# Second-layer products four steps behind the first layer instead of two, from token block 1 on

## The chip, the cores and the metric

The kernel runs on one core of one Trainium2 chip. The metric is the device time of one execution in microseconds. TensorE does the matrix products (PE, its weight loads PEld), VectorE (DVE), ScalarE (ACT) and GpSimd (POOL) the elementwise work, and SyncE (SP) issues the DMA transfers.

## The reference, cut to what matters

Causal attention with a decay, then two MLPs, all in float32. 2304 tokens in rows of 512, 32 heads of 64.

```python
x = attention(q, k, v, f)              # 4 x 8 heads, 576 tokens -> (2304, 512)
h = x @ w_in                           # first layer, 512 -> 2048
g = h * np.tanh(np.where(h > 20.0, h, np.log1p(np.exp(np.minimum(h, 20.0)))))
x2 = g @ w_out                         # second layer, 2048 -> 512
h2 = x2 @ w2_in                        # second stage, 512 -> 1024
solu = h2 * softmax(h2)
out = (layer_norm(solu) * g_ln) @ w2_out   # 1024 -> 512
```

## The kernel before

Every float32 operand is split into a high and a low half in float16, and each product is three matmuls: high by high, high by low, low by high. The tokens are worked off in nine blocks of 256 (`TB`, `NBLK`), the 2048 columns of the first MLP in 16 chunks of 128 (`NF1`). So there are 144 steps n, one for each block and chunk, and the main loop of `emit` runs over half steps `hn`.

In step n, `up(n)` is the first layer: 12 matmuls (L754) into a half of a PSUM tile `h`, which holds two steps and has two buffers (`psh`). After each pair p of steps the activation is computed in three parts. `mish_a(p)` reads `h` on ScalarE into `ta` and `th` (L766, L767; two buffers each). `mish_b(p)` does VectorE (L771), three ScalarE functions (L772 to L774) and VectorE again (L775). `mish_c(p)` casts the high half of the result on ScalarE (L780) and subtracts it on GpSimd for the low half (L781), into `gt`, of which there are three (`GB = 3`).

`down(n)` is the second layer: six matmuls (L798), three for each half of the block's tokens, that add chunk n to two PSUM banks `x2_0` and `x2_1`. Below, "product n" is the six matmuls of `down(n)`. Each bank has one buffer. After the last chunk of a block `evac` scales a bank into `x2h` (L826 on ScalarE, L827 on VectorE, one buffer) and writes it to memory (L828). The next block's first product into a bank waits for that.

Attention runs beside it in slots: scores (L410, L411, L413), exponentials on ScalarE (L454, L469), split on GpSimd (L493), a DMA transpose, and products with the values (L524 to L526). A slot also loads and converts raw tiles of q, k and v. When attention is over, the memory that it held is given to `Stage2`, which loads and splits the weights of the second stage, and the second MLP begins: `first(t)` for a tile of 128 tokens (24 matmuls, L997), normalisation, a transpose of z, `second(t)` (24 matmuls, L1037).

What decides when `down(n)` is issued is the line with `tgt` in the main loop: before, `down` follows two steps behind `up` everywhere (both branches give n - 2). A product is only issued once its `gt` exists, and `mish_c(p)` stands in step 2p + 2. The Tile framework then reorders instructions: it gives each a rank by this program order, and takes the first that is ready in its own model of the times. Each engine works off its own resulting queue in order.

Of the kernel before, what the change touches and what calls it, by code (L numbers as in the profile page):

```python
# [24 lines left out]
NF1 = DFF // P  # L25
# [15 lines left out]
WPF = 2  # L41
S2P = 1
EB = 190
DL = 2
A0 = 16
XB = 3
S2A = 10
# [160 lines left out]
def emit(tc, q, k, v, f, w_in, w_out, w2_in, w2_out, g_ln, out):  # L208
# [427 lines left out]
    def slot_pre():  # L636

        n = pos["k"] - 1
        if 0 <= n < len(seq):
            step_r(*seq[n])  # L640

    def slot_mid():
        n = pos["k"] - 1
        if 0 <= n < len(seq):
            step_h(*seq[n])
# [9 lines left out]
    def slot_pe():  # L655
        n = pos["k"]
        if n < len(seq):
            step_s(*seq[n])
            b, i, hs = seq[n]
            for h in hs:  # L660
                ahead(b, i, h)
        pvs(n - LAG)
        pos["k"] += 1

    def slot():
        slot_pre()
        slot_mid()
        if pos["k"] == n0:
            pvs(n0 - 1)
        slot_pe()  # L670
# [3 lines left out]
    for x in range(len(order) + WPF):  # L674
        if WPF <= x < len(order):
            wsteps.append((order[x][0].load, order[x][1]))
        if x >= WPF:
            w, n = order[x - WPF]
# [5 lines left out]
    def wgo(n):  # L684
        for _ in range(n):
            if wsteps:
                f, a = wsteps.pop(0)
                f(a)
                wdone.add((f, a))
# [54 lines left out]
    def up(n):  # L744
        j, fi = divmod(n, NF1)
        if fi % 2 == 0:
            hps[n // 2] = psh.tile([P, 2, TB], F32, tag="h", name=f"h_{j}_{fi}")
        ph = hps[n // 2][:, fi % 2]
        x = xT[j]
        m = 0  # L750
        for lw, lx in ((0, 0), (0, 1), (1, 0)):
            for c in range(NC1):
                col = lw * 512 + (fi % 4) * P
                nc.tensor.matmul(  # L754
                    ph, win[:, (fi // 4) * NC1 + c, col:col + P], x[:, lx * NC1 + c, :],
                    start=(m == 0), stop=(m == 3 * NC1 - 1))
                m += 1

    def mish_a(p):
        j, fi = divmod(2 * p, NF1)  # L760
        ph = hps.pop(p)
        ta = mp.tile([P, 2, TB], F32, tag="ta", name=f"ta_{p}")
        th = mp.tile([P, 2, TB], F32, tag="th", name=f"th_{p}")
        tmp[p] = (ta, th)
        for b, a, e in segs(j):
            nc.scalar.activation(ta[:, :, a:e], ph[:, :, a:e], AF.Exp, scale=usc(b, fi // 4))  # L766
        nc.scalar.activation(th, ph, AF.Copy, scale=ths[:, fi // 4:fi // 4 + 1] if j else -0.4 * HSC)  # L767

    def mish_b(p):
        ta, th = tmp[p]  # L770
        nc.vector.tensor_scalar(ta, ta, E20, 1.0, op0=ALU.min, op1=ALU.add)  # L771
        nc.scalar.activation(ta, ta, AF.Square)  # L772
        nc.scalar.activation(ta, ta, AF.Ln, scale=0.2, bias=c_k1)
        nc.scalar.activation(ta, ta, AF.Exp, scale=-1.0)  # L774
        nc.vector.scalar_tensor_tensor(th, ta, 2.5, th, op0=ALU.subtract, op1=ALU.mult)  # L775

    def mish_c(p):
        ta, th = tmp.pop(p)
        gt = mp.tile([P, 2, 2, TB], F16, tag="gt", name=f"gt_{p}", bufs=GB)
        nc.scalar.copy(gt[:, 0], th)  # L780
        nc.gpsimd.tensor_tensor(gt[:, 1], th, gt[:, 0], op=ALU.subtract)  # L781
        gts[p] = gt
# [76 lines left out]
    def att_slots(n):  # L859

        j, r = divmod(n, 2 * NF1)
        goal = cum[-1] * min(1.0, (n + 1) / EB)
        x = n0 + LAG + sum(c <= goal + 1e-6 for c in cum[1:])
        lo = need[j + 1] + LAG if j + 1 < NBLK and r >= 2 * NF1 - ATE else 0
        if j == 0:
            lo = max(lo, n0 + LAG + min(need[1] - n0, (r + 1) * (need[1] - n0) // A0))
        hi = need[j + XB] - 1 if j + XB < NBLK else len(seq) + LAG
        return min(max(x, lo), hi)

    NF = NBLK * NF1  # L870
# [1 line left out]
    done = {"d": 0}  # L872
    st2 = None

    for hn in range(2 * (NF + 5)):
        n, half = divmod(hn, 2)
        live = n < NF
        att_now = live and pos["k"] < att_slots(hn)
        if att_now:
            slot_pre()  # L880
        if half == 0:
            if n % 2 == 0 and 0 <= n // 2 - 1 < NF // 2:
                mish_b(n // 2 - 1)
            if att_now:
                slot_mid()
            if live:
                while n < NF1 and (w1_split, n // 4 * 2 + 1) not in wdone:
                    wgo(1)
                up(n)
        else:  # L890
            if live and n % 2:
                while n > NF1 and wsteps:
                    wgo(1)
                mish_a(n // 2)
            if n % 2 == 0 and 0 <= n // 2 - 1 < NF // 2:
                mish_c(n // 2 - 1)
            if att_now:
                slot_mid()
            tgt = n - 2 if (n > DL + 8 or n >= NF) else n - DL
            while done["d"] < min(tgt, NF):  # L900
                if done["d"] // 2 not in gts:
                    break
                while done["d"] < NF1 and (w2_split, done["d"] // 2) not in wdone:
                    wgo(1)
                down(done["d"])
                done["d"] += 1
        if att_now:
            slot_pe()
        wgo(WS1)
        while live and pos["k"] < att_slots(hn):  # L910
            slot()
        if half and wstp is not None and not wsteps:
            wstp.close()
            wstp = None
        if st2 is None and half and pos["k"] >= len(seq) + LAG:
            ea.close()
            st2 = Stage2(tc, es, w2_in, w2_out, g_ln, x2d, us2, out, ones)
            st2n = n
        if st2 is not None:
            if hn % S2E == 0:  # L920
                st2.prepare(S2P)
            if half and n > st2n + S2A and (n - S2A) % S2B == 0 and st2.ready():
                st2.step(TT * (done["d"] // NF1))
# [165 lines left out]
```

## Time and profile before

| | us |
|---|---|
| median of three runs | 861.46 |
| lowest and highest of them | 859.14, 862.57 |
| the profiled execution | 862.0 |
| its span in the trace | 860.2 |

| engine | busy us | share |
|---|---|---|
| TensorE (matmuls) | 748.2 | 87% |
| VectorE | 606.7 | 71% |
| ScalarE | 549.1 | 64% |
| GpSimd | 442.2 | 51% |

Busy is the time in which an engine worked on something; idle time stands before the instruction that ended it, with what released it ("<-"). Matmuls overlap, so their mean duration is longer than the time from one to the next.

### The profile page before, as it was taken

How to read it: one execution, taken by the hardware profiler on the slowest of the kernel's cores; microseconds unless marked ns; L12 is line 12 of the kernel's file. 1: busy time of each engine (PE TensorE's matmuls, PEld its weight loads, DVE VectorE, ACT ScalarE, POOL GpSimd, SP SyncE). 2: the span in 40 equal slices, each digit the busy share in tenths (PEclk: the TensorE clock that was granted, in tenths of full speed). 3: DMA queues.
4: the chain of work that ended last, by engine and by line, in shares of the span. 5: the costliest groups of instructions: out<-in, count | busy, mean ns of one | idle time of the engine just before them, and what ended most of it. 6: DMA issues, size and time to landing. Idle time of an engine off the chain costs nothing.

```text
span 860.2 us, 16457 instructions
## 1 busy us (share of the span) xinstructions
PE 748.2 (87%) x6174; PEld 477.6 (56%) x6174; DVE 606.7 (71%) x1158; ACT 549.1 (64%) x1202; POOL 442.2 (51%) x341
## 2 busy tenths in 40 slices
PE   0555777789899988999999999986999999999997
PEld 0444545557567665676757677554555554444443
DVE  6699998597667878858887755599566444665451
ACT  5555657868778786888886767686955554333331
POOL 2268676755876576776678753228733122022110
PEclk9999997789999999999999999999999999999999
DMA  9999554487897889898896632841023423344543
GB/s 237 208 246 271 166 174 92 87 157 120 149 190 157 154 152 161 178 191 140 164 184 124 138 67 56 221 172 62 26 38 79 81 59 75 89 98 104 108 88 81
DMA packets 328571, 114.88 MB, mean 134 GB/s; under 512 B 317676, under 2 KB 317676, under 8 KB 328492
## 3 DMA queue, kind: packets, MB, share of 16 engines
q1 hardware_dynamic: 328492, 113.84, 63.2%
q8 instruction: 48, 0.79, 0.4%
q14 instruction: 31, 0.25, 0.1%
HBM read 46.59 MB, written 9.55 MB: 65 GB/s over the span
## 4 chain that ended last, share of the span: by engine, by line
PE 40%; DVE 23%; DMA 13%; ACT 9%; issue 8%; POOL 7%; SPq 1%; POOLq 0%; DVEq 0%; ACTq 0%
PE h L997 10%; PE o L1037 10%; PE x L798 9%; PE h L754 7%; DMA pT<-ph 4%; POOL ph L493 4%; DVE th L775 3%; DVE ta L771 2%; DMA w2i_r<-in_moe_w_in_dram 1%; DVE wout L140 1%; PE pv L524 1%; DVE ph L490 1%; DVE wout L138 1%; POOL gt L781 1%; DMA rawk<-in_k_dram 1%
## 5 line engine op out<-in xcount | busy, mean ns | idle before, releaser
L798 PE MATMUL x<-wout,gt 128*128 128x512 f16 x864 | 222.1, 392 | 21.8 <-ACT gt L780 10.1
L754 PE MATMUL h<-xT,win 128*128 128x256 f16 x1728 | 223.3, 279 | 2.3 <-POOL win L202 1.7
L493 POOL TENSOR_TENSOR ph<-p,ph 128x512 f16<-128x512 f32 (+4 forms) x120 | 159.6, 1334 | 80.3 <-ACT ph L492 32.8
L754 PEld LDWEIGHTS <-win 128*128 128x128 f16 x1728 | 170.3, 100 | 45.3 <-POOL win L202 1.8
L781 POOL TENSOR_TENSOR gt<-th,gt 128x512 f16<-128x512 f32 x72 | 91.9, 1277 | 100.5 <-ACT gt L780 100.5
L798 PEld LDWEIGHTS <-gt 128*128 128x128 f16 x864 | 81.6, 100 | 103.7 <-issue 14.9
L1025 POOL TENSOR_TENSOR z<-sl,z 128x1024 f16<-128x1024 f32 x18 | 38.7, 2150 | 138.1 <-DVE s2c L1004 111.3
L997 PE MATMUL h<-w,x2T 128*128 128x512 f16 x432 | 98.4, 380 | 2.9 <-POOL w L205 1.6
L1037 PE MATMUL o<-wo,zT 128*128 128x512 f16 x432 | 96.5, 379 | 0.5 <-DMA zT<-z 0.5
L410 PE MATMUL sp<-kt,qa 128*128 128x128 f16 (+3 forms) x480 | 71.8, 225 | 21.1 <-ACT p L454 11.9
L454 ACT ACTIVATE p<-sp,nm 64x64 f32<-64x64 f32 (+7 forms) x128 | 61.2, 484 | 41.0 <-DVE nm L452 23.3
L524 PE MATMUL pv<-vt,pT 128*128 128x64 f16 (+3 forms) x480 | 71.0, 203 | 15.4 <-DMA pT<-ph 10.7
L775 DVE SCALAR_TENSOR_TENSOR th<-ta,th 128x512 f32<-128x512 f32 x72 | 69.4, 965 | 21.1 <-ACT ta L774 20.9
L780 ACT CAST gt<-th 128x512 f16<-128x512 f32 x72 | 44.3, 615 | 48.6 <-DVE th L775 47.2
L411 PE MATMUL sp<-kt,qb 67*128 67x128 f16 (+3 forms) x480 | 72.9, 226 | 2.6 <-DVE qb L399 2.6
L997 PEld LDWEIGHTS <-x2T 128*128 128x128 f16 x432 | 42.3, 98 | 53.9 <-issue 4.0
L525 PE MATMUL pv<-vt,pT 128*128 128x64 f16 (+3 forms) x480 | 70.1, 198 | 1.0 <-DVE vt L198 1.0
L1037 PEld LDWEIGHTS <-zT 128*128 128x128 f16 x432 | 42.2, 98 | 51.5 <-DMA zT<-z 1.0
L526 PE MATMUL pv<-vt,pT 128*128 128x64 f16 (+3 forms) x480 | 70.3, 198 | 0.0
L772 ACT ACTIVATE ta<-ta 128x512 f32<-128x512 f32 x72 | 45.3, 631 | 36.0 <-DVE ta L771 35.8
L524 PEld LDWEIGHTS <-pT 128*128 128x128 f16 (+3 forms) x480 | 45.6, 102 | 36.7 <-DMA pT<-ph 20.5
L771 DVE TENSOR_SCALAR ta<-ta 128x512 f32<-128x512 f32 x72 | 53.7, 745 | 16.6 <-ACT ta L766 16.2
(235 smaller groups left out, 1455.8 us busy)
## 6 DMA issues: line engine op xcount, KB each, us to landing
wi_r<-in_moe_w_in_dram SPq DMA_DIRECT2D x8, 1024.0 KB
wo_r<-in_moe_w_out_dram SPq DMA_DIRECT2D x8, 1024.0 KB
rawk<-in_k_dram SPq DMA_DIRECT2D x25, 256.0 KB
rawv<-in_v_dram SPq DMA_DIRECT2D x25, 256.0 KB
x2d<-x2h SPq DMA_DIRECT2D x18, 256.0 KB
out_dram<-ro SPq DMA_DIRECT2D x18, 256.0 KB
w2i_r<-in_moe_w_in_dram SPq DMA_DIRECT2D x4, 1024.0 KB
w2o_r<-in_moe_w_out_dram SPq DMA_DIRECT2D x4, 1024.0 KB
```

Source lines behind the costliest of these rows:

```text
L410: nc.tensor.matmul(o, qa[:, h, r0:r1_], kc[:, h, a0:a1], start=True, stop=False)
L411: nc.tensor.matmul(o, qb_[:67, h, r0:r1_], kc[:67, H + h, a0:a1], start=False, stop=(c != i))
L493: nc.gpsimd.tensor_tensor(p4[:, :, 1], pv3, p4[:, :, 0], op=ALU.subtract)
L524: nc.tensor.matmul(o, pT[a0:a1, k, :m], vh, start=(c == 0), stop=False)
L526: nc.tensor.matmul(o, pT[a0:a1, k + 1, :m], vh, start=False, stop=(c == i))
L754: nc.tensor.matmul(ph, win[:, (fi // 4) * NC1 + c, col:col + P], x[:, lx * NC1 + c, :], start=(m == 0), stop=(m == 3 * NC1 - 1))
L771: nc.vector.tensor_scalar(ta, ta, E20, 1.0, op0=ALU.min, op1=ALU.add)
L775: nc.vector.scalar_tensor_tensor(th, ta, 2.5, th, op0=ALU.subtract, op1=ALU.mult)
L781: nc.gpsimd.tensor_tensor(gt[:, 1], th, gt[:, 0], op=ALU.subtract)
L798: nc.tensor.matmul(o, gt[:, lg, n % 2, t * P:(t + 1) * P], wout[:, fi, lw * 512:(lw + 1) * 512], start=(first and m == 0), stop=(last and ...
L997: nc.tensor.matmul(h[:, half * 512:(half + 1) * 512], x[:, lx * NC1 + c, :], self.w2[:, half * NC1 + c, lw * 512:(lw + 1) * 512], start=(n ...
L1037: nc.tensor.matmul(o, zT[:, lz * NF2 + c, :], self.wo[:, c, lw * 512:(lw + 1) * 512], start=(n == 0), stop=(n == 3 * NF2 - 1))
```

## The change

From step 20 on (`NF1 + 4`), `down` follows four steps behind `up`; in steps 20 and 21 no product is issued while the distance grows. The constant `DL` becomes `DL2 = 4`, and the loop has two steps more at its end for the last products. Block 0's products keep their distance.

```diff
-DL = 2
+DL2 = 4
...
-    for hn in range(2 * (NF + 5)):
+    for hn in range(2 * (NF + DL2 + 3)):
...
-            tgt = n - 2 if (n > DL + 8 or n >= NF) else n - DL
+            tgt = n - 2 if n < NF1 + 4 else n - DL2
```

Since the framework orders by rank, the four queues differ from product 22 on. Three places show it. Names end in a number of the build; `gt_45` holds products 90 and 91, `h_5_14` is the first layer of block 5, chunks 14 and 15.

TensorE at product 90, before (four of its six matmuls stand ahead of the rest of `h_5_14`):

```order
L798 LDWEIGHTS gt_45_7155
L798 MATMUL x2_5_1_0_6663<-wout_94,gt_45_7155 128x512
L754 LDWEIGHTS win_93
L754 MATMUL h_5_14_7191<-xT_5_4301,win_93 128x256
L754 LDWEIGHTS win_93
```

TensorE at product 90, now (the last of its six matmuls, and what follows):

```order
L798 LDWEIGHTS gt_45_7143
L798 MATMUL x2_5_1_0_6771<-wout_94,gt_45_7143 128x512
L754 LDWEIGHTS win_93
L754 MATMUL h_6_0_7236<-xT_6_5177,win_93 128x256
L754 LDWEIGHTS win_93
```

Product 90 moved behind the whole of `h_5_14` and runs in one piece; the next block's `h_6_0` follows it.

ScalarE at the end of block 1, before (`x2h_2` and `x2h_3` empty the two banks of block 1; `qn_2_0`, `kn0` and `vt_2_0` convert raw tiles of the next batch; `nm_1_4` belongs to attention):

```order
L469 ACTIVATE p32_1_129,rsum_1_4_3318<-sp0_146,nm_1_4_1_3369 128x512
L826 ACTIVATE x2h_3_3224<-x2_1_1_0_2155,x2m_3_3218 128x512
L780 CAST gt_17_3360<-th_17_3306 128x512
L766 ACTIVATE ta_18_3445<-h_2_4_3334,usc1_0_79 128x2x64
L766 ACTIVATE ta_18_3445<-h_2_4_3334,usc1_1_80 128x2x192
```

ScalarE there, now:

```order
L767 ACTIVATE th_19_3572<-h_2_6_3458,ths_91 128x512
L197 ACTIVATE qn_2_0_3531<-rawq_2_0_3480,scu_2_3392 64x8x64
L197 ACTIVATE kn0_124<-rawk_2_0_3482,scu_2_3392 64x8x64
L197 ACTIVATE vt_2_0_3537<-rawv_2_0_3484,scv_2_3395 64x512
L826 ACTIVATE x2h_3_3350<-x2_1_1_0_2155,x2m_3_3344 128x512
L772 ACTIVATE ta_19_3571<-ta_19_3571 128x512
```

The emptying of the second bank moved from ahead of the cast of pair 17 to behind the first part of pair 19 and behind three conversions of raw tiles.

SyncE there, before (`x2d` is the write of `x2h` to memory):

```order
L300 DMA rawq_2_0_3492<-in_q_dram 64x8x64
L498 DMA_TRANSPOSE pT_1_3_6_3234<-ph_1_3_6_3164 128x16x128
L828 DMA x2d_95<-x2h_2_3212 128x1024
L300 DMA rawk_2_0_3494<-in_k_dram 64x8x64
L300 DMA rawv_2_0_3496<-in_v_dram 64x8x64
L828 DMA x2d_95<-x2h_3_3224 128x1024
```

SyncE there, now:

```order
L300 DMA rawq_2_0_3480<-in_q_dram 64x8x64
L300 DMA rawk_2_0_3482<-in_k_dram 64x8x64
L300 DMA rawv_2_0_3484<-in_v_dram 64x8x64
L828 DMA x2d_95<-x2h_2_3338 128x1024
L498 DMA_TRANSPOSE pT_1_4_0_3362<-ph_1_4_0_3294 128x20x128
L551 DMA_TRANSPOSE xT_3_2923<-xh_1_3_3427 128x8x128
L396 DMA_TRANSPOSE qa_2_0_3534<-qn_2_0_3531 128x8x64
L300 DMA rawq_2_1_3775<-in_q_dram 128x8x64
L374 DMA_TRANSPOSE kt_2_0_3527<-kn0_124 128x8x64
L300 DMA rawk_2_1_3777<-in_k_dram 128x8x64
L828 DMA x2d_95<-x2h_3_3350 128x1024
```

The first write moved behind two raw loads and the second behind six more issues.

## Rows read from the trace of the kernel before

**Rows 1.** The page's head: span, busy us, share and instructions of each engine.

```profile
span 860.2 us, 16457 instructions
PE 748.2 (87%) x6174; PEld 477.6 (56%) x6174; DVE 606.7 (71%) x1158; ACT 549.1 (64%) x1202; POOL 442.2 (51%) x341
```

**Rows 2.** Windows: stretch and length, busy us of PE, PEld, DVE, ACT, POOL, PEclk, DMA.

```profile
0.00:237.00 237.00, 158.49 (x1488) 115.44 (x1489) 195.44 (x334) 154.73 (x348) 147.88 (x107) 0.91 0.78 173
237.00:537.00 300.00, 284.07 (x3043) 201.35 (x3042) 222.01 (x415) 232.82 (x562) 198.10 (x178) 0.99 0.80 147
537.00:606.00 69.00, 55.80 (x362) 35.14 (x360) 57.59 (x90) 49.94 (x88) 28.42 (x18) 0.98 0.47 145
606.00:856.00 250.00, 249.52 (x1288) 125.64 (x1285) 131.71 (x320) 110.90 (x206) 67.84 (x40) 1.00 0.37 77
```

**Rows 3.** Groups of TensorE, 237 to 537: count, busy us, mean ns, idle before, releasers.

```profile
L754 PE MATMUL h<-xT,win 128*128 128x256 f16 x888 | 114.8, 274 | 0.0
L798 PE MATMUL x<-wout,gt 128*128 128x512 f16 x434 | 110.1, 384 | 8.6 <-ACT gt L780 5.2 <-POOL gt L781 2.7 <-DVE x2h L827 0.5
L524 PE MATMUL pv<-vt,pT 64*128 64x64 f16 (+2 forms) x330 | 48.0, 197 | 6.2 <-DMA pT<-ph 5.1 <-DVE nm L452 0.8
```

**Rows 4.** Waits of TensorE, 237 to 537: who for whom, us in total, times, longest.

```profile
PE x L798 <- ACT gt L780: 5.2, 8, 1.3
```

**Rows 5.** Timeline of TensorE: start us, us, instruction, count, [idle before, releaser].

```profile
288.21 1.04 PE L798 MATMUL x<-wout,gt 128*128 128x512 f16 x4 [1.28 <-ACT gt L780]
...
335.51 1.04 PE L798 MATMUL x<-wout,gt 128*128 128x512 f16 x4 [1.00 <-ACT gt L780]
...
405.67 1.90 PE L798 MATMUL x<-wout,gt 128*128 128x512 f16 x8 [0.41 <-POOL gt L781]
...
418.53 1.89 PE L798 MATMUL x<-wout,gt 128*128 128x512 f16 x8
...
426.96 2.76 PE L798 MATMUL x<-wout,gt 128*128 128x512 f16 x12
...
434.45 3.56 PE L798 MATMUL x<-wout,gt 128*128 128x512 f16 x8 [1.97 <-POOL gt L781]
...
515.78 1.04 PE L798 MATMUL x<-wout,gt 128*128 128x512 f16 x4 [0.77 <-ACT gt L780]
```

**Rows 6.** Windows: the three stretches of a lower granted clock behind 237 us.

```profile
253.61:257.02 3.41, 3.41 (x22) 2.48 (x20) 3.38 (x6) 2.24 (x5) 3.05 (x4) 0.50 0.91 197
434.52:437.93 3.41, 3.41 (x10) 1.22 (x11) 2.57 (x7) 3.41 (x8) 2.60 (x3) 0.50 1.24 238
594.94:598.35 3.41, 2.69 (x7) 0.98 (x7) 3.41 (x6) 0.84 (x2) 2.13 (x2) 0.50 0.20 77
```

**Rows 7.** Groups of TensorE, 537 to 606.

```profile
L798 PE MATMUL x<-wout,gt 128*128 128x512 f16 x112 | 28.2, 389 | 9.1 <-ACT gt L780 4.1 <-DVE x2h L827 3.8 <-POOL gt L781 1.2
```

**Rows 8.** The chain that ended last, 534 to 612: shares by line.

```profile
by line: DMA w2i_r<-in_moe_w_in_dram 16.3%; issue 11.2%; DMA w2o_r<-in_moe_w_out_dram 8.2%; DVE wo L138 5.6%; DVE wo L146 5.5%; DVE th L775 5.0%; PE x L798 4.7%; DVE w L138 4.7%; DVE wo L140 4.3%; DMA xT<-xh 4.1%; DVE ta L771 3.8%; DVE us L
```

**Rows 9.** Waits of ScalarE, 237 to 537.

```profile
ACT gt L780 <- DVE th L775: 20.8, 20, 1.9
...
ACT x2h L826 <- DMA x2d<-x2h: 2.1, 2, 1.1
```

**Rows 10.** Timelines of TensorE and SyncE (SPq: an issue) in the last stretch.

```profile
723.42 5.34 PE L997 MATMUL h<-w,x2T 128*128 128x512 f16 x24
...
735.07 1.46 PE L798 MATMUL x<-wout,gt 128*128 128x512 f16 x6
736.37 5.34 PE L997 MATMUL h<-w,x2T 128*128 128x512 f16 x24
741.55 5.34 PE L1037 MATMUL o<-wo,zT 128*128 128x512 f16 x24
...
742.36 2.04 SPq L1027 DMA_TRANSPOSE zT<-z  x1
```

**Rows 11.** The chain that ended last, in order: start us, us, what.

```profile
846.52 4.40 DMA zT<-z
```

## The prediction, made blind

> **What bounds the kernel now.** I read the page first, then the busy time of each engine by stretch, then TensorE's groups and waits inside the stretch that the change touches, then the single rows with a wait. The profiled execution took 862.0 us, of which the trace spans 860.2; the median of the three runs is 861.46, so whatever the trace gives is lowered by 0.54 us at the end. TensorE is busy for 748 of 860 us and no other engine comes near [rows 1]. Cut at 237, 537 and 606 us, the trace shows four stretches [rows 2]. Up to 237 us (block 0 and the first half of block 1) TensorE is busy for two thirds and its clock is at 0.91. From 237 to 537 us attention runs beside blocks 1 to 5 and TensorE is busy 284.07 of 300 us. From 537 to 606 us the weights of the second stage are loaded and split, and it is busy 55.80 of 69. From 606 us on it is busy 249.52 of 250. The last stretch is pure queue: it can only start earlier, not get shorter. So what the change is worth is what it does to the waits between 237 and 606 us.
>
> In the 300 us before 537 the first-layer products (L754) never wait: 888 matmuls, idle 0.0. The second-layer products (L798) do: 8.6 us, of which 5.2 for the cast of gt on ScalarE, 2.7 for its low half on GpSimd, 0.5 for a PSUM bank. The attention products (L524) wait another 6.2 us, most of it (5.1) for transposes [rows 3]. 888 matmuls are 74 steps of 12, so a step lasts 300/74 = 4.05 us here. That is the time that each step of lag buys.
>
> **The change, part by part.** *Before the divergence.* The engines' orders are the same up to product 21, so nothing before about 237 us changes: 0 us.
>
> *The wait for gt.* Counting from TensorE's order how many first-layer products stand ahead of a second-layer product (its number taken off), the lag was 4.0 to 5.8 in the steady parts of blocks 1 to 6 and is now 6.0. The scheduler had let some products slide already, which is why it is not two steps everywhere. The waits of the steady parts are the eight on the ScalarE cast, 5.2 us with 1.3 as the longest [rows 4]. The first large one is at 288.21 (product 36, lag 4.1, now 8.0), the last at 515.78 (90, 5.6, now 6.0) [rows 5]. Seven of the eight move by at least 0.4 of a step, 1.6 us, which is longer than any of these waits. Product 46 at 335.51 moves by 0.2, 0.8 us of its 1.0. I count all eight as gone. The two large waits for GpSimd's half are different: 0.41 at 405.67 (product 62) and 1.97 at 434.45 (product 68) [rows 5]. There the lag was already 6.4 and 7.9, and is now 6.0 and 6.9; I leave both as they are. The 0.5 for the bank and 0.2 for another instruction stay as well. So of 8.6 us, 8.6 - 1.97 - 0.41 - 0.5 - 0.2 = 5.5 go. What is late next is TensorE's own queue: first-layer products are always ready, and the attention products behind come earlier by the same amount, as do the scores that start their chain. If instead those chains set the pace, the 5.5 turn up as longer waits on L524. The ends of this term are therefore 0 and -8.6; I take -5.5, since TensorE is busy 95% of the stretch, ScalarE 78%, VectorE 74%, GpSimd 66% [rows 2].
>
> *The clock.* Three stretches of 3.41 us at half speed lie behind 237 us, from 253.61, 434.52 and 594.94 on, granted 0.50, which is the lower of the two levels, 1.2 GHz. Each costs up to 3.41 x 0.5 = 1.7 us [rows 6]. The second begins at the wait of 1.97 us, and the third at the bank's wait of 3.8 in the weights' stretch. The longest wait that I remove, 1.28 us at 288.21, brought no drop with it [rows 5, 6], so this term is 0; its other end is -5.1. The Trainium skill (TensorE: Matmul & The Clock Gate, A second HAM failure mode) says that small pauses between groups of matmuls can by themselves make the clock swing. The trace does not bear this out here, as the pauses for the cast of up to 1.3 us [rows 4] left the clock alone between the first two drops; by the rule, 1.7 us more would come back for each drop that goes.
>
> *The weights' stretch, 537 to 606 us.* L798 waits here 4.1 us for the cast, 3.8 for a PSUM bank and 1.2 for GpSimd [rows 7]. But the chain of waits through this stretch runs over the weight loads and the conversion on VectorE, and second-layer products have 4.7% of it [rows 8]. Product 106 goes from lag 6.0 to 6.2 and product 108 from 8.0 to 6.2: 1.8 steps of queue less ahead of the latter, each 114.8/74 = 1.55 us of first-layer work [rows 3]. I take 0, with -4.1 (the cast waits go) and +2.8 (1.8 x 1.55, product 108 reached earlier and nothing else to do) as ends.
>
> *Queues moved past.* SyncE's write of x2h to memory for block 1 now stands behind two raw loads, and the second one behind six more issues; on ScalarE the second x2h now stands behind three conversions of raw tiles. Their price shows where x2h waited before: ScalarE 2.1 us in two waits in the 300 us [rows 9]. It delays only product 33, which itself moves from lag 6.2 to 11.0; cover is the four steps, 16 us, in between. 0 us, up to +2.1 without cover.
>
> *The tail.* After the last first-layer product TensorE still has four or more second-layer products instead of two; the same work, in a full queue: 0. Seven products of output tile 7 now stand ahead of score tile 9. Before, the 24 score products of tile 7 began at 723.42; 24 such last 5.18 us (736.37 to 741.55), so they ended at 728.6. Its transpose was issued at 742.36 [rows 10] and the kernel's last one took 4.40 to land [rows 11], so zT was there at 746.8, 18.2 us after. In the new order three groups of 24 and three second-layer products of 1.30 us (735.07 to 736.37) lie between: 15.5 + 3.9 = 19.4 us. It just fits: 0, up to +1.5.
>
> Sum: -5.5 us. 862.0 - 5.5 = 856.5 for a profiled execution, **856.0** against the median.
>
> **The rivals.** *Held buffers (slower).* There are three gt tiles. A product that stands late holds its tile, and the cast of the pair three further on waits for it on ScalarE, in whose queue the exponentials of attention stand behind. It decides once a lag passes about 9, which happens where a block begins and its second bank comes free late. What such a place costs can be read at block 4 before: product 64 at 418.53, 65 at 426.96 (lag 10.9), then the wait of 1.97 [rows 5] and the half-speed stretch of 1.7 [rows 6], 3.7 us. The second bank's product now stands later at four block starts: 33 (6.2 to 11.0), 49 (7.3 to 8.9), 81 (6.2 to 7.8), 97 (8.4 to 10.2). Four times 3.7 less 5.5 is +9.3, three times +5.6: 866.5 to 870.2, say 869. Against it: the scheduler put the casts behind, and two of the four stay under 9. Perfetto Trace Analysis of the Trainium skill (Optimization Strategy) reads a repeating gap on the engine that should be full as a possible lack of tiles for the next step. By that reading the waits for gt would not go with a longer lag at three tiles; the rows speak against it, as the casts themselves waited 20.8 us for VectorE in 20 places [rows 9] and no wait of theirs for L798 stands among them.
>
> *Given back (no change).* The chains of attention set the pace between 237 and 537 us, and L524's 6.2 us grow by what L798 loses. For it: five of the 6.2 are waits for transposes, which no second-layer product holds up [rows 3]. It gives 861.5, and 859 where half is given back.
>
> *More goes.* The large waits go too: all 8.6 us, and the two clock drops at 253.61 and 434.52: 8.6 + 3.4 = 12.0 us, 849.5. For it: fewer cuts, since TensorE's order falls from 695 runs of like products to 661. Against it: nothing moves the lags of 62 and 68 the right way.
>
> *It does not do what it says.* In part that is so (products 62 to 69 and 106 to 111 are not later), and it is in the sum.
>
> **How the numbers follow.** Forecast 856.0: 0.36, its own range 852 to 860. More goes: 0.16. Given back: 0.28. Held buffers: 0.20. A measurement of this kernel can tell about 0.5%, 4.3 us, so faster means below 857.2 and slower above 865.8. The forecast's case falls in faster for nine tenths (0.32) and in same for the rest (0.04); more goes adds 0.16 to faster: 0.48, same 0.32, slower 0.20. The range must leave out at most 0.2: from the middle of "more goes" with the ends of the clock and the weights' stretch (849.5 less 3.5) at 846 to the lower half of "held buffers" at 868.
>
> **What would show it.** Right: in the stretch with attention the wait of L798 on the cast falls from 5.2 to under 1.5 us, L524's stays near 6, the attention ends some 5 us before 537, and the last stretch is 250 us long as before. Wrong by buffers: ScalarE's cast waiting for L798, at the starts of blocks 2 to 6. Wrong by giving back: L524 or L410 waiting longer by what L798 lost. Wrong in the weights' stretch: first-stage products waiting more than 4 us for split weights. If the order, shuffled on every engine behind product 22, meets chains that the rows of before do not show, all of these fail together.

## The result: 1.46% slower, and where the trace shows it

The changed kernel takes 874.49 us (median of 4, 873.75 to 874.60) against 862.02 us before (median of 4, 859.14 to 863.27): a ratio of 1.0146, 95% interval 1.0124 to 1.0167. The prediction was 856.0 with a range of 846 to 868: wrong in sign, and outside its range. The profiled run of the changed kernel took 874.53 us with a span of 872.7; the span of before is 860.2 [rows 1]. So 12.5 us are to be found.

The same four stretches of the changed kernel, with the columns of [rows 2] (length, busy us of PE, PEld, DVE, ACT, POOL, PEclk, DMA):

```profile
0.00:237.00 237.00, 155.60 (x1499) 114.12 (x1500) 198.29 (x335) 155.98 (x351) 146.04 (x107) 0.88 0.77 174
237.00:537.00 300.00, 280.93 (x3006) 200.95 (x3004) 226.11 (x404) 228.65 (x555) 201.94 (x176) 0.98 0.82 146
537.00:606.00 69.00, 52.57 (x339) 33.15 (x338) 58.74 (x81) 45.41 (x80) 29.41 (x17) 0.94 0.47 142
606.00:856.00 250.00, 248.40 (x1282) 126.16 (x1282) 139.01 (x340) 117.98 (x217) 68.39 (x41) 0.99 0.35 75
```

In both middle stretches TensorE does less in the same time (280.93 for 284.07, 52.57 for 55.80) at a lower granted clock (0.98 for 0.99, 0.94 for 0.98). TensorE's groups from 237 to 537 us, beside [rows 3]:

```profile
L754 PE MATMUL h<-xT,win 128*128 128x256 f16 x860 | 111.3, 275 | 0.0
L798 PE MATMUL x<-wout,gt 128*128 128x512 f16 x432 | 110.9, 387 | 1.7 <-POOL gt L781 1.5 <-DVE x2h L827 0.2
L524 PE MATMUL pv<-vt,pT 64*128 64x64 f16 (+2 forms) x330 | 48.5, 198 | 14.8 <-DMA pT<-ph 14.2 <-DVE x L539 0.4
```

The first step came true: the waits for the ScalarE cast, 5.2 us before, are gone. But L524's waits went from 6.2 to 14.8 us, and all of that growth is for transposed probabilities. More was given back than was won.

Below, the trace is cut by work and not by time. The **attention stretch** runs from the first product with V of chunk 2 of batch 1 to that of the last head pair of batch 3 (before: 235.1 to 532.6 us); the **rest** runs from there to the second stage's last output tile. TensorE's order gives each matmul its product. The 12.5 us are then -1.2 ahead of the attention stretch (where the orders are alike), +3.5 in it (297.6 to 301.1) and +10.2 in the rest (318.3 to 328.5).

In the rest, two waits at the start of block 7 stand out, in TensorE's timeline of the changed kernel:

```profile
591.60 4.41 PE L754 MATMUL h<-xT,win 128*128 128x256 f16 x24 [2.33 <-ACT th L767]
...
606.63 2.72 PE L798 MATMUL x<-wout,gt 128*128 128x512 f16 x6 [8.46 <-DVE x2h L827]
```

The second is product 112, block 7's first, which waits until block 6's bank is emptied: 8.46 us, where before the whole stretch from 537 to 606 us had 3.8 of that kind [rows 7]. All of TensorE's waits in the rest are 18.8 us, 13.6 before. VectorE tells why. Between the reduction of the bank (L820) and the subtraction that frees it (L827) it works on the second stage's output weights (tile wo) and on GELU steps (tile ta):

```profile
589.62 0.68 DVE L820 TENSOR_REDUCE x2m<-x 128x1 f32<-128x512 f32 x1
590.23 2.92 DVE L146 TENSOR_SCALAR wo<-wo,gl 128x512 f32<-128x512 f32 x2
593.07 0.13 DVE L821 TENSOR_SCALAR x2m<-x2m 128x1 f32<-128x1 f32 x1
593.13 2.55 DVE L136 TENSOR_SCALAR wo<-w2o_r 128x1024 int32<-128x1024 int32 x1
595.60 0.14 DVE L253 TENSOR_SCALAR x2m<-x2m 128x1 int32<-128x1 int32 x1
595.66 1.31 DVE L771 TENSOR_SCALAR ta<-ta 128x512 f32<-128x512 f32 x1
596.89 2.05 DVE L138 SCALAR_TENSOR_TENSOR wo<-w2o_r,wo 128x1024 int32<-128x1024 int32 x1
598.87 0.15 DVE L823 RECIPROCAL x2m<-x2m 128x1 f32<-128x1 f32 x1
598.94 2.00 DVE L840 SCALAR_TENSOR_TENSOR us<-x2m,kb 128x1 f32<-128x1 f32 x1
600.86 1.21 DVE L140 SCALAR_TENSOR_TENSOR wo<-w2o_r,wo 128x1024 int32<-128x1024 int32 x1
602.00 0.14 DVE L824 TENSOR_SCALAR x2m<-x2m 128x1 f32<-128x1 f32 x1
602.06 1.20 DVE L771 TENSOR_SCALAR ta<-ta 128x512 f32<-128x512 f32 x1
603.18 2.73 DVE L146 TENSOR_SCALAR wo<-wo,gl 128x512 f32<-128x512 f32 x2
605.83 0.74 DVE L827 SCALAR_TENSOR_TENSOR x2h<-x,x2m,x2h 128x512 f16<-128x512 f32 x1
```

That is 16.2 us from one to the other. Before, the same pair:

```profile
583.24 0.68 DVE L820 TENSOR_REDUCE x2m<-x 128x1 f32<-128x512 f32 x1
...
594.87 0.74 DVE L827 SCALAR_TENSOR_TENSOR x2h<-x,x2m,x2h 128x512 f16<-128x512 f32 x1
```

11.6 us, with one pair of L146 less and one L775 in place of two L771. The clock falls too. The windows of the changed kernel's half-speed stretches behind 237 us (columns as above):

```profile
591.55:594.96 3.41, 3.36 (x16) 2.31 (x16) 3.41 (x4) 2.23 (x4) 3.24 (x3) 0.50 0.02 5
601.79:612.03 10.24, 5.40 (x18) 2.57 (x18) 9.39 (x18) 7.48 (x13) 4.90 (x4) 0.50 0.13 51
267.29:270.70 3.41, 3.41 (x27) 1.85 (x26) 1.72 (x4) 3.41 (x10) 1.26 (x2) 0.50 1.35 227
308.25:315.08 6.83, 6.31 (x50) 4.39 (x47) 5.58 (x9) 4.68 (x17) 5.33 (x6) 0.50 1.13 155
407.24:410.65 3.41, 3.41 (x20) 1.87 (x17) 2.91 (x9) 2.40 (x9) 3.00 (x3) 0.50 1.16 215
```

27.3 us in five stretches, 13.65 in the attention stretch and 13.65 in the rest, where before had 6.83 and 3.41 [rows 6]. Each begins in a wait of TensorE or shortly behind one: that at 407.24, for example, behind this.

```profile
405.24 0.20 PE L524 MATMUL pv<-vt,pT 64*128 64x64 f16 x1 [1.77 <-DMA pT<-ph]
```

### The profile page after: what moved, and what is told of

It reads as the page before. It is cut to its first block, busy times and chain, and to the rows that moved or that the text cites. A ratio compares the mean times of both kernels' runs of the same rounds, so it can differ in the third digit from the quotient of the medians.

```text
span 872.7 us, 16476 instructions
## 1 busy us (share of the span) xinstructions
PE 749.2 (86%) x6174; PEld 479.3 (55%) x6174; DVE 622.2 (71%) x1158; ACT 550.1 (63%) x1202; POOL 447.8 (51%) x341
## 4 chain that ended last, share of the span: by engine, by line
PE 37%; DVE 24%; DMA 13%; ACT 11%; issue 9%; POOL 5%; SPq 1%; DVEq 0%; ACTq 0%; POOLq 0%
PE o L1037 10%; PE h L997 10%; PE h L754 7%; PE x L798 6%; DMA pT<-ph 6%; DVE th L775 3%; POOL ph L493 2%; DVE ta L771 2%; DMA w2i_r<-in_moe_w_in_dram 1%; DVE wout L140 1%; PE pv L524 1%; DMA qa<-qn 1%; ACT p L454 1%; ACT p L469 1%; DVE nm L452 1%
## 5 line engine op out<-in xcount | busy, mean ns | idle before, releaser
L798 PE MATMUL x<-wout,gt 128*128 128x512 f16 x864 | 220.1, 390 | 21.1 <-DVE x2h L827 9.6
L754 PE MATMUL h<-xT,win 128*128 128x256 f16 x1728 | 227.3, 282 | 6.3 <-ACT th L767 3.9
L754 PEld LDWEIGHTS <-win 128*128 128x128 f16 x1728 | 172.9, 102 | 54.1 <-issue 7.2
L781 POOL TENSOR_TENSOR gt<-th,gt 128x512 f16<-128x512 f32 x72 | 95.5, 1327 | 106.4 <-ACT gt L780 105.2
L798 PEld LDWEIGHTS <-gt 128*128 128x128 f16 x864 | 82.3, 100 | 99.9 <-issue 17.1
L775 DVE SCALAR_TENSOR_TENSOR th<-ta,th 128x512 f32<-128x512 f32 x72 | 69.8, 969 | 37.7 <-ACT ta L774 36.7
L524 PE MATMUL pv<-vt,pT 128*128 128x64 f16 (+3 forms) x480 | 70.6, 202 | 25.0 <-DMA pT<-ph 22.4
L524 PEld LDWEIGHTS <-pT 128*128 128x128 f16 (+3 forms) x480 | 45.1, 101 | 46.8 <-DMA pT<-ph 31.6
L771 DVE TENSOR_SCALAR ta<-ta 128x512 f32<-128x512 f32 x72 | 55.5, 770 | 13.8 <-ACT ta L766 13.4
```

Of the source, the lines that this page charges most:

```text
L524: nc.tensor.matmul(o, pT[a0:a1, k, :m], vh, start=(c == 0), stop=False)
L754: nc.tensor.matmul(ph, win[:, (fi // 4) * NC1 + c, col:col + P], x[:, lx * NC1 + c, :], start=(m == 0), stop=(m == 3 * NC1 - 1))
L798: nc.tensor.matmul(o, gt[:, lg, n % 2, t * P:(t + 1) * P], wout[:, fi, lw * 512:(lw + 1) * 512], start=(first and m == 0), stop=(last and ...
```

## The experiments

Three questions: which stretch loses, what in it, and whether the lag or the order that the scheduler makes of it is to blame. In the diffs, - is the changed kernel unless another is named. Each kernel was timed beside the kernel before (median 860.1 us in e1 to e4, 861.1 in e5 to e8, 860.5 in e9 to e12, 860.1 in e13 to e16). The letters are those of the expectations; H is another theory in e12 than in e7, and G2 in e13 another than G.

**e1, e2: one half of the change at a time.**

```
e1: -            tgt = n - 2 if n < NF1 + 4 else n - DL2
    +            tgt = n - DL2 if NF1 + 4 <= n < 6 * NF1 else n - 2
e2: +            tgt = n - DL2 if n >= 6 * NF1 else n - 2
```

> Lag of four only in blocks 1 to 5 (first-layer products 20 to 95), back to two from product 96 on: the attention stretch is that of the changed kernel, the stretch in which the second stage's weights are converted has the old lag. Theory A (the loss is made in the weights' stretch, where VectorE's order puts more conversion steps between the reduction x2m_12 and the subtraction x2h_12 and product 112 waits 8.46 us instead of 3.82): here VectorE's order has two conversion-free steps in between, so product 112 waits under 4 us, and the kernel gives 860 to 866 us, the 2 us that the attention stretch lost included. Rival B (the loss comes of the attention stretch, which ended 2.3 us later, and of the buffers held there): about 872 to 875 us. Rival C (the greater lag in the last blocks costs as such): 859 to 863 us.

> Lag of two up to first-layer product 95, lag of four from 96 on: the attention stretch is mostly that of before, the weights' stretch has the greater lag. Here VectorE's order between x2m_12's reduction and x2h_12 holds one conversion step's end (one L140 and a pair of L146) and two of the GELU steps L771, fewer than before's seven and after's seven plus two. Theory A (VectorE's order decides, the lag only reshuffles it): product 112 waits 1 to 5 us and the kernel gives 860 to 867 us. Rival B (attention stretch): 859 to 863 us. Rival C (the greater lag in the last blocks costs as such, since the banks of block 6 are emptied two products later): 869 to 874 us.

e1: 866.60 us, ratio 1.0074 (1.0050 to 1.0098), 0.6 above theory A's range. e2: 864.32, 1.0050 (1.0034 to 1.0067), inside it; product 112 waited 3.25 us there, and in e1 under 0.15. So each half loses, and the attention stretch more than A had allowed; of the rivals, B's and C's ranges for e2 (859 to 863 and 869 to 874) both fail. TensorE's groups in that window, first of e1, then of e2:

```profile
L798 PE MATMUL x<-wout,gt 128*128 128x512 f16 x429 | 110.0, 387 | 1.9 <-POOL gt L781 1.5 <-DVE x2h L827 0.4
L524 PE MATMUL pv<-vt,pT 64*128 64x64 f16 (+2 forms) x330 | 48.7, 199 | 14.8 <-DMA pT<-ph 14.1 <-DVE x L539 0.5
```

```profile
L798 PE MATMUL x<-wout,gt 128*128 128x512 f16 x438 | 110.5, 383 | 9.0 <-ACT gt L780 5.0 <-POOL gt L781 3.4 <-DVE x2h L827 0.5
L524 PE MATMUL pv<-vt,pT 64*128 64x64 f16 (+2 forms) x330 | 48.0, 197 | 5.4 <-DMA pT<-ph 5.1 <-DVE x L539 0.3
```

e1 has the changed kernel's pattern and e2 that of before, each in its own execution: the swap of one wait for the other belongs to the lag in blocks 1 to 5 and not to chance. The attention stretch took 302.3 us in e1 and 296.4 in e2.

**e3, e4: the weights earlier, in both kernels.**

```
e3, e4: -S2E = 3
        +S2E = 2
```

> The changed kernel with the second stage's weight steps handed out every second half step instead of every third (S2E = 2). VectorE's order then has all conversion steps but one L136 ahead of or behind the stretch from x2m_12's reduction to x2h_12. Theory A: product 112 waits under 4 us instead of 8.46, and against its control (the kernel before with the same S2E) it loses at most 5 us, where the change lost 12.5. Rivals B and C: it loses 10 to 14 us against its control, as the change did.

> The control: the kernel before with S2E = 2. VectorE's order keeps a pair of L146, a whole conversion step (L136, L138, L140) and one L775 between x2m_12's reduction and x2h_12, as with S2E = 3. Theory A: product 112 waits 3 to 6 us and the kernel gives 859 to 867 us. Rivals B and C say nothing different of it; it is what the run of the changed kernel with S2E = 2 is compared with.

e4: 863.55 us, with a wait of product 112 of 2.33 us where 3 to 6 had been expected. e3: 869.95, that is 6.4 more than its control where A allowed 5 and the rivals 10 to 14. TensorE's timeline of e3 at block 7:

```profile
599.96 0.59 PE L754 MATMUL h<-xT,win 128*128 128x256 f16 x2 [4.69 <-ACT th L767]
601.85 2.72 PE L798 MATMUL x<-wout,gt 128*128 128x512 f16 x6 [1.30 <-DVE x2h L827]
```

Product 112's wait fell from 8.46 to 1.30 as A said, but 4.69 us moved to the product ahead of it, which waits for a bank that the GELU's second read (L767 on ScalarE) still holds. The rest took 323.3 us against 322.2 in the control, so the 10.2 us of the change shrink to 1.1. The attention stretch took 302.6 against 296.3.

**e5, e6: the row scale off VectorE, in both kernels.**

```
e5, e6: -                nc.vector.tensor_scalar(
        -                    f[:, s], f[:, s], self.row_scale[:, 2 * n + s:2 * n + s + 1], None, op0=ALU.mult)
        +                nc.scalar.activation(
        +                    f[:, s], f[:, s], AF.Copy, scale=self.row_scale[:, 2 * n + s:2 * n + s + 1])
```

> The changed kernel with the row scale of the second stage's output weights (L146, eight 128x512 multiplications on VectorE, 2.92 and 2.73 us for the two pairs that stood between x2m_12's reduction and x2h_12) done on ScalarE. VectorE's order then has one L771, one L136 and one L775 in between. Theory A (VectorE's order in the weights' stretch makes about 8 of the 12.5 us, the attention stretch the rest): product 112 waits under 3 us instead of 8.46, and the kernel gives 863 to 868 us. Rival B (the attention stretch alone): 872 to 876 us. Rival C (the greater lag in the last blocks as such): 871 to 875 us.

> The kernel before with the same row scale on ScalarE: nothing but one L140 and x2m_12's own steps stands between x2m_12's reduction and x2h_12. Product 112 waits under 2 us instead of 3.82. Theory A: 855 to 861 us, so that against it the changed kernel with this edit loses 4 to 7 us, what the attention stretch lost. Rivals B and C: it loses 10 to 14 us.

e6: 860.0 us (ratio 0.9994, 0.9974 to 1.0015). e5: 870.5 (866.5 to 872.1), 10.5 more; A had said 4 to 7. Product 112 waits again, for something else:

```profile
601.46 1.04 PE L798 MATMUL x<-wout,gt 128*128 128x512 f16 x2 [4.62 <-ACT gt L780]
```

The work taken off VectorE's queue stands in ScalarE's, ahead of the cast, and holds that queue for 3.05 us, until VectorE's L140 has written the tile. The rest: 325.0 us against 317.5. So theory A holds for the 8.46 us as such, the wait for the bank follows VectorE's order, but removing it does not give the time back: other waits take its place.

**e7, e8: less work for TensorE in the attention stretch.** In blocks 1 to 5 one matmul of six is left out of each second-layer product but the last of a block, 71 in all, some 15 us.

```
e7 (of before), e8 (of after):
-            for m, (lg, lw) in enumerate(((0, 0), (0, 1), (1, 0))):
+            for m, (lg, lw) in enumerate(((0, 0), (0, 1), (1, 0))[:2 if t and 20 <= n < 96 and not last else 3]):
```

> The kernel before with one matmul of six left out of the second-layer products 20 to 95, but for the last of each block: 71 matmuls, some 15 us of TensorE's work gone from the attention stretch. It leaves out a part of the product of the second layer. Theory G (in the attention stretch TensorE's time is given back: a wait that goes turns up as a longer wait for the next transposed probabilities, since the chain from the scores over the exponential, the split and the transposing transfer to the product with V has a time of its own): the last attention product starts at most 6 us earlier than before's 532.6 us, and the waits for the transposed probabilities (5 us in before) grow by 6 us or more. Rival H (TensorE's work bounds the stretch, and the longer lag lost time for another reason): it starts 12 to 16 us earlier and those waits stay under 8 us.

> The same matmuls left out of the changed kernel. Theory G: the last attention product starts within 5 us of where it does in the changed kernel (534.9 us), with waits for transposed probabilities of 18 us and more instead of 13.9. Rival H: it starts 12 to 16 us earlier, and those waits stay at 12 to 16 us.

e7: 860.25 us, level with before (ratio 0.9988, 0.9966 to 1.0009), though 15 us of work are gone. Its attention stretch took 295.0 us, 2.6 less than before's profile. TensorE's products with V from 237 to 537 us, in e7:

```profile
L524 PE MATMUL pv<-vt,pT 64*128 64x64 f16 (+2 forms) x330 | 49.1, 200 | 10.3 <-DMA pT<-ph 10.2
```

The waits of the stretch grew from 15.8 to 23.3 us and its half-speed time from 6.8 to 17.1. That is theory G, but that the waits for transposes grew by 5 us and not by 6. e8: 851.5 us, its attention stretch 283.3 instead of 301.1, 17.8 less, more than the work that went, with 15.6 us of waits. That is theory H, but that the waits for transposes fell from 13.9 to 9.6 us and did not stay at 12 to 16. Neither theory holds for both: the same 15 us of work are worth 2.6 us in one order of the engines and 17.8 in the other.

**e9, e10: the scores four slots ahead.**

```
e9 (of after), e10 (of before): -LAG = 3
                                +LAG = 4
```

> The changed kernel with the scores four slots ahead of the products with V instead of three (LAG = 4), so that the chain from a slot's scores to its product with V has the time of four slots. Seen so far: from the first reduction of a slot to its product with V 12.7 to 13.0 us pass in every kernel of either lag, and the waits for transposed probabilities grew from 5 to 14 us when the waits for the ScalarE cast went. Theory G (the waits were given back because the chain's time is set and TensorE arrives at it earlier): with a fourth slot the waits for transposed probabilities fall below 7 us between the first product with V of chunk 2 of batch 1 and the last one of batch 3, and that stretch, 301 to 302.6 us in the changed order, falls to 293 to 298 us. Rival O (the scheduler's new order of the engines loses the time, and the chain's length does not matter): 299 to 304 us, waits of 10 us and more.

> The control: the kernel before with LAG = 4. Theory G: its waits for transposed probabilities, 5 us, fall below 3, the waits for the ScalarE cast stay at 4 to 6, and the stretch takes 293 to 297 us instead of 296 to 298; the changed kernel with LAG = 4 is then level with it or up to 4 us shorter in this stretch. Rival O: the changed kernel's stretch stays 3 to 6 us longer than this one's.

e9: 866.58 us, its stretch 301.2 with 10.7 us of waits for transposes, where G had said under 7 and at most 298. e10: 859.94, stretch 298.7, 7.4 us, where G had said 293 to 297 and under 3; its waits for the cast are 0.9 us and not 4 to 6. Rival O holds for e9's stretch and waits; for the difference between the two it had said 3 to 6 us, and it is 2.5. G's reading of a chain with a fixed time fails: with a fourth slot the mean from the end of the last reduction behind a transpose to the first product with V that uses it grew from 12.9 us (after) and 12.7 (before) to 13.2 (e9) and 13.7 (e10). What hardly changed is the part up to the issue of the transfer, 6.9 to 7.3 us in the mean of each of the four; in the changed kernel a product with V of chunk 3 or 4 that waits starts 4.3 us or more behind the issue of its transfer. So a fourth slot lets more pass between the two ends, but the waits fell by 3 us only.

**e11 to e14: other lags.**

```
e11, e12, e13: -DL2 = 4
               +DL2 = 3, 6, 5
               -            tgt = n - 2 if n < NF1 + 4 else n - DL2
               +            tgt = n - DL2 if NF1 + 4 <= n < 6 * NF1 else n - 2
e14:           -DL2 = 4
               +DL2 = 6
```

> A lag of three in blocks 1 to 5 only, two elsewhere. Theory G: between the lags of two and four, with waits for the ScalarE cast of 1 to 4 us and for transposed probabilities of 6 to 12 us; the stretch of the attention takes 297 to 301 us and the kernel 860 to 866 us. Rival O (what the scheduler's order happens to be): anything from 293 to 304 us, with no relation to the lag.

> A lag of six in blocks 1 to 5 only, two elsewhere. Theory G: no waits for the cast, waits for transposed probabilities of 10 to 16 us as with the lag of four, the stretch 299 to 304 us and the kernel 864 to 870 us. Rival H (the longer the GELU's output tiles are held, three of them, the more is lost): waits of first-layer products and of casts for free tiles appear, and the stretch takes over 305 us, the kernel over 871 us. Rival O: anything from 293 to 304 us.

> A lag of five in blocks 1 to 5 only, two elsewhere. Theory O (no trend with the lag; the stretch is TensorE's work of 276 to 279 us, plus its waits of 15 to 20 us, which are given back at any lag, plus half of the half-speed time that the longer single waits happen to bring): the stretch takes 292 to 303 us, and this sum gives it to 2 us. Rival G2 (the lag itself costs, and six was an exception of its own): 300 to 304 us with 13 us and more at half speed, as at three and four.

> The change with a lag of six instead of four in all blocks after block 0. Theory O: the attention stretch is that of the lag of six in blocks 1 to 5, 291 to 295 us, and in the weights' stretch VectorE's order has only two GELU steps and no conversion step between x2m_12's reduction and x2h_12, so product 112 waits under 4 us: 855 to 863 us. Rival C (the greater lag in the last blocks costs as such, more with six than with four): from the last attention product to the end 326 us or more instead of 318, and 862 to 872 us.

Lag three: 869.27 us (ratio 1.0089, 1.0060 to 1.0117), its profiled run the fastest at 865.7; both its time and its stretch of 302.2 us lie above G's ranges, and O had allowed the stretch. Five: 867.90 (1.0088, 1.0072 to 1.0103), its attention stretch of 298.6 us with 6.8 at half speed as O allowed and G2 did not; the loss is in the rest. Six in blocks 1 to 5: 862.29 (1.0011, 0.9995 to 1.0027), no loss that can be measured, and outside what G and H had said; its stretch of 292.9 lies 0.1 below O's. Six in all blocks: 863.16 (1.0041, 1.0022 to 1.0059), just above O's range and inside C's. Product 112 does not wait there, but the rest took 326.6 us: at block 6's start a second-layer product now waits 8.52 us for its bank, and a sum that belongs to the output weights (L953) waits 7.56 us for VectorE. The products with V in this window, for lags three, five and six (e11, e13, e12):

```profile
L524 PE MATMUL pv<-vt,pT 64*128 64x64 f16 (+2 forms) x330 | 48.7, 199 | 12.6 <-DMA pT<-ph 10.9 <-DVE x L539 1.5
```

```profile
L524 PE MATMUL pv<-vt,pT 64*128 64x64 f16 (+2 forms) x330 | 48.2, 198 | 12.5 <-DMA pT<-ph 12.3
```

```profile
L524 PE MATMUL pv<-vt,pT 64*128 64x64 f16 (+2 forms) x330 | 47.8, 197 | 12.8 <-DMA pT<-ph 12.8
```

**e15, e16: candidates, lag six in blocks 1 to 5 with the weight work moved.** Both start from e12: e15 with the row scale of e5, e16 with S2E = 4.

> A lag of six in blocks 1 to 5, two elsewhere, and the row scale of the output weights on ScalarE. Theory O: the attention stretch 291 to 295 us, product 112 waits under 3 us, and from the last attention product to the end 318 to 324 us: 853 to 861 us. Rival: the ScalarE work delays the casts and the last blocks lose what was gained, 862 to 868 us.

> A lag of six in blocks 1 to 5, two elsewhere, with the weight steps handed out every fourth half step (S2E = 4). VectorE's order has no conversion step between x2m_12's reduction and x2h_12. Theory O: the attention stretch 291 to 295 us, product 112 waits under 3 us, from the last attention product to the end 318 to 324 us: 853 to 861 us. Rival: the second stage's weights come too late, and its products wait: 862 to 870 us.

862.52 us (1.0027, 1.0013 to 1.0041) and 862.31 (1.0035, 1.0020 to 1.0050). Both are just above theory O's range and in the rivals': the attention stretches were as expected, 292.6 and 294.6, but the rests took 326.3 and 324.9 us instead of at most 324, though product 112 waited under 3 us in both, as expected. Nothing that was tried beats the kernel before, but for the kernel that leaves work out.

**All in one table**, in us, from TensorE's rows of each profile. "Cast" and "pT": its waits for the ScalarE cast and for transposed probabilities; "half": time at the lower clock level; all within the attention stretch. The wait right ahead of the stretch's last product, up to 0.8 us, is not counted. Each row is one profiled execution, in e11 3.5 us and in e12 2.7 us faster than the kernel's median.

| kernel | lag in blocks 1 to 5, 6 to 8 | stretch | cast | pT | all waits | half | rest |
|---|---|---|---|---|---|---|---|
| before | 2, 2 | 297.6 | 5.2 | 5.2 | 15.8 | 6.8 | 318.3 |
| e2 | 2, 4 | 296.4 | 5.0 | 5.1 | 16.0 | 3.4 | 321.7 |
| e4 | 2, 2 | 296.3 | 5.6 | 7.2 | 18.1 | 0 | 322.2 |
| e6 | 2, 2 | 296.3 | 4.6 | 4.8 | 15.3 | 6.8 | 317.5 |
| after | 4, 4 | 301.1 | 0 | 13.9 | 18.5 | 13.7 | 328.5 |
| e1 | 4, 2 | 302.3 | 0 | 13.5 | 18.1 | 17.1 | 321.8 |
| e3 | 4, 4 | 302.6 | 0 | 12.6 | 19.5 | 13.7 | 323.3 |
| e5 | 4, 4 | 300.7 | 0 | 10.2 | 16.5 | 17.1 | 325.0 |
| e11 | 3, 2 | 302.2 | 0.9 | 10.3 | 17.9 | 13.7 | 319.2 |
| e13 | 5, 2 | 298.6 | 0 | 12.1 | 20.1 | 6.8 | 324.8 |
| e12 | 6, 2 | 292.9 | 0 | 12.0 | 16.5 | 3.4 | 323.6 |
| e14 | 6, 6 | 291.5 | 0 | 10.0 | 14.4 | 6.8 | 326.6 |
| e15 | 6, 2 | 292.6 | 0 | 8.7 | 13.4 | 10.2 | 326.3 |
| e16 | 6, 2 | 294.6 | 0 | 11.3 | 16.5 | 6.8 | 324.9 |
| e10, scores 4 ahead | 2, 2 | 298.7 | 0.9 | 7.4 | 16.3 | 13.7 | 321.7 |
| e9, scores 4 ahead | 4, 4 | 301.2 | 0.9 | 10.7 | 20.3 | 10.2 | 323.2 |

Read it by groups, without e9 and e10. Lag two: 296.3 to 297.6. Lag four: 300.7 to 302.6, four executions, none near the others. That is 301.7 against 296.7 in the mean: **+5.0 us**, where the prediction had -5.5. At every lag above two the cast's waits go, but for 0.9 us at three, and the transposes' grow, so that all waits together move little: 15.3 to 18.1 at lag two, 13.4 to 20.1 with longer lags (18.2 in the mean of lag four, 16.3 of lag two). What differs more between the lags is the time at half speed: 0 to 6.8 us at two, 13.7 to 17.1 at three and four, 3.4 to 10.2 at five and six. But it does not order the kernels by itself: within a lag the stretch does not follow it, and e10 has 13.7 us at half speed with the lag of two, e9 10.2 with four, and e9 is the longer. Take waits and half of the half-speed time off the stretch, and 277.6 to 278.7 us remain at lag two and 275.7 to 276.3 at four (some of the waits lie inside the half-speed time and are taken off twice). At lag six the stretch looks 4 us shorter in the mean, but three of the four kernels with it have 25 first-layer matmuls fewer in it, 2.9 us at 24 in 2.78 us, which come later (the rest is longer by them), and e14 has nine second-layer ones fewer. Lag six neither wins nor loses.

## Why the prediction was wrong, point by point

**Before product 22: 0.** Right. The stretch up to the first product with V of chunk 2 ended at 233.9 instead of 235.1 us, and the other kernels with the scores three slots ahead, which are the same up to there, had it at 231.4 to 236.7.

**The wait for gt: -5.5.** The first half of the step was right: all waits for the cast went in the changed kernel, e1, e3 and e5. The second half failed, "what is late next is TensorE's own queue". I chose it over the end that I had named, the chains of attention, by the busy shares of the engines. These are averages and say nothing of a chain that is late once in each slot. In the changed kernel L524 waits instead of L798: 14.2 us for transposes, 5.1 before. The mean time from the end of the last reduction behind a transpose to the first product with V that uses it is 12.7 us before and 12.9 after, over the 48 transposes of the stretch. That fits a TensorE that comes sooner to probabilities that do not. It is not a proof, since the scores that start the chain are TensorE's too, and in e7 the same mean is 13.8. One rival had no run of its own: that the transposes wait for one of the two buffers of pT (`PTB = 2`), which the products with V set free. SyncE's rows speak against it, first before, then after (us, times, longest, 237 to 537):

```profile
SPq L498 <- PE pv L526: 7.0, 6, 2.2
```

```profile
SPq L498 <- PE pv L526: 0.6, 1, 0.6
```

Its other waits ahead of a transpose are for GpSimd's work. ScalarE shows the giving back one step further up. Its exponentials waited for the buffer that GpSimd's subtraction frees, before:

```profile
ACT p L454 <- POOL ph L493: 4.1, 7, 1.9
```

and after, from the same view (us, times, longest):

```profile
ACT p L454 <- POOL ph L493: 10.6, 11, 2.7
```

In e1 it is 8.6 us, in e2 4.1 as before; at lag six (e12) it is 5.8, with waits for transposes almost as long. So a part of the removed casts' slack was passed up the chain at lag four, but this step alone does not explain the waits, and which engine holds the chain stays open. With the lag of two a giving back is shown by e7 too, 15 us of work gone and 2.6 won; e8 shows that it does not hold in every order.

**The clock: 0, other end -5.1.** Wrong, and the end was on the wrong side: I bounded below and did not ask what new waits would do. Half-speed time in the attention stretch rose by 6.8 us against before's profile and by 11.1 in the mean of four against four, worth up to half of that, 3.4 and 5.5 us. By the table 1.9 us of the +5.0 are longer waits. If the work in the stretch is the same, 3.1 us are left for the 11.1 at half speed, 0.28 us for each; this is a sum and no run tests it. The Trainium skill (TensorE: Matmul & The Clock Gate, A second HAM failure mode) says that small pauses between groups can make the clock swing. The prediction set it against the trace because eight pauses of up to 1.3 us had brought no drop; here, with waits of 0.8 to 1.8 us at the products with V, the trace agrees with it. It does at the lag of two as well: in e6 the same pause for the cast at product 36 lasted 1.38 us instead of 1.28, and a stretch of 3.41 us at a granted clock of 0.50 began as it ended (TensorE's timeline, then the window). One execution of the kernel before was too little to rule the drops out.

```profile
288.55 1.89 PE L798 MATMUL x<-wout,gt 128*128 128x512 f16 x4 [1.38 <-ACT gt L780]
288.51:291.92 3.41, 3.37 (x12) 1.80 (x13) 1.67 (x6) 2.15 (x5) 1.22 (x1) 0.50 0.66 142
```

Whether lags of three and four lead into such drops and those of five and six do less so by a rule, or by how the scheduler's order falls, stays open: no run holds the clock fixed or separates it from the waits.

**The weights' stretch: 0, ends -4.1 and +2.8.** Wrong: +10.2 us in the rest. The step that failed took the lag as all that the change does there and costed product 108. The loss sits at product 112, which I had left alone because its lag stays at 8. What moved was VectorE's order around block 6's bank (16.2 us from reduction to release, 11.6 before) and TensorE's time at half speed, 13.65 for 3.41. In other orders the greater lag costs here 1.1 (e3 less e4), 3.4 (e2 less before) and 7.5 us (e5 less e6), and e1, with the lag of two in these blocks, loses 3.5 to before. So the cost of the greater lag here depends on the order, and the runs do not settle how much of the 10.2 is the lag's own.

**Queues moved past: 0, up to +2.1.** No sign against it: ScalarE's x2h waited 0.5 us for the write of the one before, 2.1 before [rows 9].

**The tail: 0, up to +1.5.** Right within 0.6: output tile 17's wait for its transpose is 1.07 us, 0.48 before. From score tile 8 to there 115.2 us pass, 114.6 before.

**The rivals.** "Given back" had the mechanism of the attention stretch, at 0.28, but not its sign. "Held buffers" had the nearest number, 866.5 to 870.2 (its own terms, +5.6 and +9.3 on 861.46, give 867.1 to 870.8), and the wrong mechanism: no cast of the changed kernel waits for L798 between 237 and 537 us. At lag six, which holds the tiles longest, two casts do wait for it (e12: 2.4 us in all), and the kernel loses nothing. The last sentence of the prediction, an order shuffled on every engine that meets chains which the rows of before do not show, is what happened; it was given no time and no chance of its own.

## What to carry to other kernels

A wait that goes is worth its time only if what TensorE meets next is ready; ask for each engine's next chain what it costs from its first step to its use, not how busy the engines are. Where a scheduler orders by readiness, a change of one number is a new order on every engine: e7 and e8 value the same edit at 2.6 and 17.8 us of the attention stretch, so such a change deserves a range with both signs, and a scan of the number before a verdict on it. And a wait traded for another of the same sum can still lose: of the attention stretch's 24 waits 4 were over 1.2 us before and 7 after, and TensorE's time at half speed doubled, though no run here isolates what that costs.

## What the hardware showed that I had not expected

Some of VectorE's instructions get longer while GpSimd works. In the listing above L136 takes 2.55 us, L840 (128x1) 2.00 and a pair of L146 2.92. Alone, L136 took 0.68 to 0.70 us in six of eight cases of the changed kernel between 537 and 612 us, and L840 0.14 elsewhere. GpSimd's timeline at that time:

```profile
596.66 1.22 POOL L202 TENSOR_SCALAR w<-w 128x1024 f16<-128x1024 f32 x1
597.96 2.96 POOL L205 TENSOR_TENSOR w<-w 128x1024 f16<-128x1024 f32 x1
601.01 1.97 POOL L202 TENSOR_SCALAR w<-w 128x1024 f16<-128x1024 f32 x1
```

Of these four lines, the rows without GpSimd beside them have one duration each, and those with it are up to 14 times as long (in us, 537 to 612: L136 0.69 to 2.55, L146 0.47 to 2.34, L771 0.42 to 1.38, L840 0.14 to 2.00). Not all are hit: the reduction L820 takes 0.67 to 0.69 us with GpSimd beside it and without. The Trainium skill (Trainium Architecture — The Big Picture, What this means for kernel authors) says that these two engines share a pair of ports under an exclusive lock; the rows of the four lines agree, that of L820 does not show it. So the 16.2 us ahead of x2h_12 are partly GpSimd's splitting of the first weights, which no table of VectorE's own durations shows.
